# A gated-attention block with an MLP on one core: a fourth round of the second MLP product in three reduced passes, attention results parked in DRAM, and a new order of the work

## The chip, the cores and the metric

The kernel runs on one core of a Trainium2 chip. The metric is device time in microseconds (us) of one execution; lower is better. Kernels are compared by the median of several executions. The trace comes from one further, profiled execution.

## What is computed

The first half is a recurrent attention (four batches, eight heads, 768 time steps, 48 channels per head). Its output is laid out as 768 rows of 384 numbers per batch, and a normalized MLP with a residual follows, 384 to 1536 to 384.

```python
for t in range(S):
    kt, vt, rt, wt = (k[:, :, t], v[:, :, t], r[:, :, t], w[:, :, t])
    cur = np.einsum('bhd,bhe->bhde', u[None] * kt, vt)
    y[:, :, t] = np.einsum('bhd,bhde->bhe', rt, state + cur)
    state = wt[:, :, :, None] * state + np.einsum('bhd,bhe->bhde', kt, vt)
x = y.transpose(0, 2, 1, 3).reshape(B, S, H * D)
xn = (x - mu) / np.sqrt(var + 1e-06) * g_ln
out = x + np.maximum(xn @ w_ch1, 0.0) @ w_ch2
```

All inputs and outputs are 32-bit floats.

## The kernel before

The work is cut into eight rounds (four batches, two halves of 384 steps each). `front` (L1559) emits one round of attention: it loads w, k, r with `load` (L494, SyncE queue, three DMAs each), turns them with TensorE (`turn`), and then treats each chunk of 64 steps in six levels. At every level `quads` (L677) makes many small 48-row matmuls on quarters of the array, `grow` (L709) multiplies k and r by running products of w on VectorE, and `keep` copies the wanted squares out of PSUM on VectorE. `states` carries the state over the chunks, and `outputs` (L955) makes the attention result. Its last step on VectorE, `add` (L1006), writes the round's `x`, 128 x 3 x 384 numbers, 576 KB.

`back` (L1628) emits a round's MLP: `normalize` (L1030) on VectorE, `turn_x` (L1098) to transpose, and `mlp` (L1452). For rounds 1 to 7 the first product (`h_ps`, `hd_ps`) is made in three reduced-precision passes (type fp32r in the trace): the 32-bit numbers are split into a high and a low part and a correction, so that one 32-bit product is the sum of three passes. The third part of the weights, `d`, is streamed from DRAM for each of the twelve slices f of 128 hidden channels (`stream`, L1319). Round 0 uses plain 32-bit matmuls. The second product exists in two forms. Plain: for each third i of the round's rows, twelve 32-bit matmuls 128x128x384 into tile `o` (L1519 to L1555), one VectorE add (`x<-o,x`), and a store. In three passes: `thirds` (L1336), which splits h into `hH`, `hL`, `hD` (one ScalarE step, two VectorE steps per f), makes three fp32r matmuls per i and f against the split weights `w2h`, `w2l`, `w2d` that `halve2` (L1276) prepares once, and needs two VectorE steps per third at the end. `thirds` accumulates in six PSUM tiles, four of them in the two large "a" tiles that attention also uses, so it can only run when all attention is done: its first matmul waits for the `x` of the last round (L1414 to L1415). Before the change `LAST = NR - 3 = 5` (L427): rounds 5, 6 and 7 take three passes, rounds 0 to 4 are plain.

The order of the work is not the order of the text. Each step is added to a `Plan` (L67) with an engine, a cost, a due number (`pri`, smaller is more urgent), the tiles that it reads and writes, and how long after its end the result is usable (`lat`). `Plan.order` (L142) then simulates the engines and writes down one order per engine, which the chip follows strictly. `SHIFTS` (L90) moves the due numbers of single stages, and `PATIENCE`, `STAY`, `MARGIN`, `FETCH` and `WAIT` (L82 to L86) steer the choice: `STAY` is how many due numbers it is worth not to switch TensorE between the small 48-row matmuls and full-size ones. While TensorE has nothing to do in the first 90 us by the plan, `idle` matmuls are put in. Buffers are counted in `HOMES` (L330): three for `x`.

SyncE issues nearly all DMAs, in the plan's order; an entry that waits holds up all behind it.

Of the kernel before, what the change touches and what calls it, by code (L numbers as in the profile page):

```python
# [10 lines left out]
F32 = mybir.dt.float32  # L11
# [24 lines left out]
class InOrder:  # L36


    waits, last = [], None
# [27 lines left out]
class Plan:  # L67
# [11 lines left out]

    HOP, MARGIN, FILLED, PATIENCE, STAY = 0.1, 0.196918, 60.0, 4.33011, 6.79752  # L82
    BEFORE, PIECE, FETCH, CROWD = 66, 256, 3.98109, 300
    WAITS = 1.006
    DRAIN = {True: 0.1, False: 0.12}
    WAIT = {"PE": 0.0354766, "ACT": 0.217982, "DVE": 0.140393, "POOL": 0.485775, "SP": 0.0207245}  # L86

    SHIFTS = {  # L90
        -537: -0.5, -535: -6.5, -520: -4, -457: -8, -337: 9.5, -296: 10.5, -295: 5.5, -200: -2,
        -38: -71, -34: 42.5, -31: -47, -30: -6.5, -29: 16, -25: -3, -18: -10.5, -14: -56, 0:
        -25, 6: -19.5, 8: -4, 9: -2.5, 10: -43, 11: 16, 12: -24, 14: 3, 16: 18, 17: 31, 26: -27,
        46: 6.5, 50: -49, 52: 46.5, 61: -28.5, 64: 5.5, 66: 11, 68: -8, 86: 5.5, 91: -28, 96:
        -20.5, 98: -50, 102: 40.5, 110: 4.5, 121: -4, 122: 14, 125: -0.5, 127: -9, 131: -17.5,
        136: -30, 140: 24.5, 165: -9, 166: -6, 168: -11.5, 172: -40, 174: -34.5, 178: -1.5, 180:
        -14.5, 182: 25.5, 202: 4.5, 203: 37, 204: -10, 210: -66.5, 212: -41, 260: -1.5, 261:
        -16.5, 280: 30, 283: -13, 284: -4.5, 310: 5, 319: -7.5, 320: 9, 402: 6, 407: -20.5, 409:
        -6, 411: -30, 418: -9.5, 425: 2.5, 440: -68, 442: 5, 443: 5.5, 444: -9.5, 450: -20.5,
        453: 38, 459: -24, 463: 40.5, 480: 3.5, 481: 3, 483: 9.5, 486: -3.5, 490: 3.5, 495: 15,  # L100
        496: 18, 497: 17.5, 499: 64.5, 501: 5,
    }

    def __init__(self, homes, dynamic):
# [176 lines left out]
def kernel(  # L281
# [13 lines left out]
    PE, ACT, DVE, POOL, SP = (  # L295
        InOrder(tc, e) for e in (nc.tensor, nc.scalar, nc.vector, nc.gpsimd, nc.sync)
    )

    B, H, S, D = r.shape
    P = 128  # L300
# [5 lines left out]
    U = H // NH  # L306
    TT = 3
# [10 lines left out]
    NR = B * NHALF  # L318
    G = 3
    pairs, both_units = range(NP), range(U)  # L320
# [4 lines left out]
    scratch = ctx.enter_context(tc.tile_pool(name="scratch", bufs=1, space=DRAM))  # L325
# [3 lines left out]

    HOMES = {  # L330
        "nat": 5, "w": 1, "k": 2, "r": 2, "tot": 1, "decay": 3, "rk": 1, "own": 2, "own_row": 1,
        "v": 2, "vx": 2, "vo": 2, "s": 2, "last": 3, "rx": 2, "sx": 2, "x": 3, "xn": 3,
        "xf": 2, "stats": 2, "mv": 2, "rstd": 2, "raw": 4, "rest": 8, "h": 12, "w1": 4, "wl": 4,
        "w2": 12, "A": 2,
    }
# [3 lines left out]
    def tile_(tag, name, shape, dtype=F32):  # L339
        if name in tiles:  # L340
            return tiles[name]
        if tag == "a":
            tiles[name] = a_homes[plan.place[name]]
            return tiles[name]
        if tag == "nat" and name.startswith("nat_"):
            tiles[name] = nat_homes[plan.place[name]]
            return tiles[name]
        if tag == "b":
            t = banks.tile([P, 512], dtype, tag=f"b{plan.place[name]}", name=name)
            tiles[name] = t[:, 0 : shape[1]]  # L350
            return tiles[name]
        t = homes.tile(shape, dtype, tag=f"{tag}{plan.place[name]}", name=name)
        tiles[name] = t
        return t
# [25 lines left out]
    for i in range(2):  # L380
        plan.hold("A", f"A{i}")
        a_bufs.append(tile_("A", f"A{i}", [P, 2, U, NK, C]))
    own_d = [scratch.tile([RN, H], F32, name=f"own_d{i}") for i in range(ROWS)]
    w1_d = scratch.tile([FC, P, KC, P], F32, name="w1d")
    masks = [const.tile([P, C // 2], I8, name=f"mask{lev}") for lev in range(NLEV - 1)]
# [38 lines left out]

    BY = {"DVE": DVE, "POOL": POOL}
    EITHER = ("DVE", "POOL")
    THREE, LAST = 1, NR - 3  # L427

    def at(rnd, stage):
        return 40 * rnd + stage  # L430

    EVICT, CONVERT, FILL = -1000, 38, 200

# [8 lines left out]
    def urgent(part, stage):  # L444
        rnd, c0, nc = part
        return at(rnd - (nc == 1), stage)
# [47 lines left out]
    def load(nm, q):  # L494
        b, f, g = units[q]
        name = f"nat_{nm}{q}"

        def go():
            to = tile_("nat", name, None)
            if q // U < ROWS:  # L500
                SP.dma_start(
                    out=to[:, 0 : NH * ROW].rearrange("p (h x) -> p h x", h=NH),
                    in_=SRC[nm][b, ts(g, NH), ds(f * RN, RN)]
                    .rearrange("h (p c) d -> p h (c d)", p=P),
                )
                return
            for c in range(TT):
                SP.dma_start(
                    out=by_tile(to)[:, c, :, 0:D],
                    in_=SRC[nm][b, ts(g, NH), ds(f * RN + c * P, P)].rearrange("h p d -> p h d"),  # L510
                )

        cost_, size = (0.5, 1.05) if q // U < ROWS else (1.65, 1.6)
        plan.add(
            "SP", cost_, go, w=[name], new=[("nat", name)], pri=at(q // U, "wrk".index(nm)), lat=2.0,
            size=size,
        )

# [308 lines left out]
    def load_v(q, part):  # L827
        _, c0, nc = part
        b, f, g = units[q]
        name, swapped = f"v{q}", f"vx{q}"  # L830

        def go():
            t = tile_("v", name, [P, NH, TT, D])
            for c in range(c0, c0 + nc):
                SP.dma_start(
                    out=t[:, :, c],
                    in_=v[b, ts(g, NH), ds(f * RN + c * P, P)].rearrange("h p d -> p h d"),
                )

        def swap():  # L840
            t, src = tile_("vx", swapped, [P, NP, TT, D]), tiles[name]
            cols = slice(c0 * D, (c0 + nc) * D)
            for i in range(2):
                SP.dma_start(
                    out=t[ds(C * (1 - i), C)].rearrange("p r c d -> p r (c d)")[..., cols],
                    in_=src[ds(C * i, C)]
                    .rearrange("p (r j) c d -> p r j (c d)", j=2)[:, :, 1, cols],
                )

        share = nc / TT  # L850
        plan.add(
            "SP", 0.1 + 1.6 * share, go, w=[(name, c0)], new=[] if c0 else [("v", name)],
            pri=urgent(part, 16), lat=2.0, size=1.6 * share,
        )
        plan.add(
            "SP", 1.3, swap, r=[(name, c0)], w=[(swapped, c0)], new=[] if c0 else [("vx", swapped)],
            pri=urgent(part, 17), lat=2.2, size=0.2 + 0.5 * share,
        )
# [96 lines left out]
    def outputs(q, before, part):  # L955
        rnd, c0, nc = part
        uu = q % U
        b, f, g = units[q]
        y_, x_, sx, s_, rx = f"y{q}_{c0}", f"x{rnd}", f"sx{q}", f"s{q}", f"rx{q}"
        tiles_of = [(pr, c) for pr in pairs for c in range(c0, c0 + nc)]  # L960

        def go():
# [36 lines left out]
            + [(f"vx{q}", c0), (f"v{q}", c0), (s_, c0), (s_, 0)]  # L999
            + [(t, j, c0) for t in (rx, sx) for j in range(2)]  # L1000
            + keys_of("r", part, [uu]) + ([before] if before else []),
            w=[y_], new=[("a", y_)] + ([("x", x_)] if uu == c0 == 0 else []), pri=urgent(part, 24),
            lat=0.17, tiled=True, count=64 * nc - 16 * (before is None and c0 == 0),
        )
        for j in range(2):
            def add(j=j):  # L1006
                x = tile_("x", x_, [P, TT, H, D])
                y = tiles[y_][:, j, 0 : NK * D].rearrange("p (r c e) -> p r c e", r=NP, c=TT)
                cs = slice(c0, c0 + nc)
                DVE.tensor_tensor(  # L1010
                    out=x[:, cs, ts(g, NH)].rearrange("p c (r j) e -> p j r c e", j=2)[:, j],
                    in0=y[:, :, cs],
                    in1=tiles[f"vo{q}"].rearrange("p (r j) c e -> p j r c e", j=2)[:, j, :, cs],
                    op=ALU.add,
                )
            plan.add(
                "DVE", cost(part, 0.12, 0.41), add, r=[y_, (f"vo{q}", c0)], w=[(x_, uu, j, c0)],
                pri=urgent(part, 24),
            )

    def x_of(rnd, tile_no=None):

        return [
            (f"x{rnd}", uu, j, c0) for _, c0, nc in parts_of_round(rnd)
            if tile_no is None or c0 <= tile_no < c0 + nc for uu in both_units for j in range(2)
        ]
# [307 lines left out]
    def thirds(rnd, f):  # L1336
# [34 lines left out]
        for i in range(TT):  # L1371
# [40 lines left out]
            keys = [o + n if i == 2 else (o, n) for n in "PD"]  # L1412
            need = [H_, L_, D_, f"w2d{f}", (f"w2h{g}", c), (f"w2l{g}", c)]
            if first:  # L1414
                need += x_of(NR - 1)  # L1415
            plan.add(
                "PE", 0.525, both, count=6, r=need, w=keys,
                new=[("a" if i < 2 else "b", n) for n in names] if first else [],
# [140 lines left out]
    def front(part):  # L1559
# [59 lines left out]
        befores = [states(q, part) for q in qs]  # L1619
        for q, before in zip(qs, befores):  # L1620
            outputs(q, before, part)

    def norm(part):
        normalize(part)
        for kc in range(KC):
            turn_x(part, kc)

    def back(rnd):  # L1628
        norm((rnd, 0, TT))
        mlp(rnd)  # L1630

# [66 lines left out]
```

## Time and profile before

| | us |
|---|---|
| median of 3 runs | 527.17 |
| lowest, highest | 525.99, 527.70 |
| profiled execution | 526.92 |
| its span in the trace | 525.20 |
| TensorE busy | 515.8 |
| VectorE busy | 403.6 |
| ScalarE busy | 269.8 |
| GpSimd busy | 72.2 |

The profiled execution took 526.92 us, of which the trace spans 525.20; 1.72 us lie around the span. Busy time is the time in which at least one instruction of an engine runs. TensorE's instructions overlap in a pipeline, so a busy share near 100% does not say that every instruction went through as fast as it could; the distance from one start to the next tells that. Granted TensorE clock is 1.00 throughout.

### The profile page before, as it was taken

The numbers are of one execution on the slowest core, as the hardware profiler recorded it, in microseconds if no ns is written. First come the engines' busy times: TensorE is split into PE (matmuls) and PEld (weight loads), VectorE is DVE, ScalarE is ACT, GpSimd is POOL, SyncE is SP. The second block draws the span as 40 slices with busy tenths as digits, with TensorE's granted clock in tenths as the row PEclk, the third lists the DMA queues.
The fourth block names the chain that finished last, engine by engine and source line by source line (L and its number), as shares of the span: only waits on it lengthen the run. The fifth ranks groups of instructions, "written<-read, shape, count | busy, mean of one in ns | idle before, by whom it ended". The sixth has DMA issues, their size and how long they took to land.

```text
span 525.2 us, 20616 instructions
## 1 busy us (share of the span) xinstructions
PE 515.8 (98%) x8996; PEld 434.5 (83%) x8996; DVE 403.6 (77%) x845; ACT 269.8 (51%) x602; POOL 72.2 (14%) x106
## 2 busy tenths in 40 slices
PE   9999999999999999999999999999999999999996
PEld 6788788677998668989777898669967999999996
DVE  5899988998899998999893886736664855855645
ACT  3788978973584244385451395246731524332221
POOL 7311311100420012223120010001500000000000
PEclk9999999999999999999999999999999999999999
DMA  9958595087545724655712311404101322322201
GB/s 215 273 158 205 119 232 163 18 208 209 143 83 102 187 50 93 145 121 102 174 39 67 78 38 25 133 22 120 47 16 61 107 61 65 101 60 85 83 0 46
DMA packets 122362, 55.84 MB, mean 106 GB/s; under 512 B 93984, under 2 KB 119200, under 8 KB 122272
## 3 DMA queue, kind: packets, MB, share of 16 engines
q1 hardware_dynamic: 119152, 53.54, 40.3%
q10 hardware_dynamic: 3120, 0.98, 1.0%
q8 instruction: 71, 1.16, 0.9%
q14 instruction: 19, 0.16, 0.1%
HBM read 45.05 MB, written 7.10 MB: 99 GB/s over the span
## 4 chain that ended last, share of the span: by engine, by line
PE 88%; DMA 4%; DVE 3%; POOL 2%; ACT 1%; issue 0%; SPq 0%; POOLq 0%; DVEq 0%
PE a L50 24%; PE o L50 23%; PE h_ps L50 21%; PE hd_ps L50 9%; PE o_2P L50 2%; PE w_ps L50 2%; PE r_ps L50 2%; DMA nat<-in_w_dram 2%; PE kn_ps L50 2%; PE k_ps L50 2%; PE xT_ps L50 1%; PE o_2D L50 1%; DVE x L50 1%; DMA own<-own_d 1%; DVE w L50 1%; POOL wide L50 1%
## 5 line engine op out<-in xcount | busy, mean ns | idle before, releaser
L50 PE MATMUL o<-ffn,h 128*128 128x384 f32 x360 | 124.4, 490 | 0.0
L50 PEld LDWEIGHTS o<-ffn,h 128*128 128x128 f32 x360 | 65.7, 190 | 37.5
L50 ACT COPY h<-hd_ps 128x384 f32<-128x384 f32 x84 | 40.3, 479 | 80.0 <-PE hd_ps L50 77.4
L50 DVE SCALAR_TENSOR_TENSOR h<-h_ps,h 128x384 f32<-128x384 f32 x84 | 46.5, 555 | 42.1 <-PE h_ps L50 38.1
L50 PEld LDWEIGHTS a<-r,k 48*60 48x60 f32 (+5 forms) x4608 | 63.3, 126 | 15.4 <-issue 7.4
L50 PE MATMUL a<-r,k 48*60 48x32 f32 (+5 forms) x4608 | 69.6, 212 | 0.9 <-issue 0.6
L50 PE MATMUL h_ps<-xhl,wl 128*128 128x384 f32 x252 | 61.1, 350 | 0.0
L50 PE MATMUL h_ps<-xhl,wh 128*128 128x384 f32 x252 | 57.6, 337 | 0.0
L50 PE MATMUL hd_ps<-xd,d 128*128 128x384 f32 x252 | 57.2, 348 | 0.0
L50 DVE TENSOR_TENSOR k<-k,tot 112x768 f32<-112x768 f32 (+1 forms) x50 | 41.7, 833 | 16.7 <-PE a L50 13.9
L50 PEld LDWEIGHTS hd_ps<-xd,d 128*128 128x128 f32 x252 | 44.2, 188 | 1.6 <-ACT w L50 0.2
L50 PEld LDWEIGHTS h_ps<-xhl,wl 128*128 128x128 f32 x252 | 43.8, 188 | 1.8 <-DVE h L50 0.2
L50 PEld LDWEIGHTS h_ps<-xhl,wh 128*128 128x128 f32 x252 | 45.2, 188 | 0.0
L50 ACT ACTIVATE h<-h 128x384 f32<-128x384 f32 x48 | 25.1, 525 | 33.3 <-DVE h L50 32.7
L50 DVE TENSOR_TENSOR r<-r,tot 112x768 f32<-112x768 f32 (+1 forms) x50 | 40.3, 807 | 0.0
L50 DVE COPY_PREDICATED A<-mask,a 128x768 f32<-128x768 int8 (+2 forms) x36 | 39.3, 1091 | 0.5 <-PE a L50 0.3
L50 ACT ACTIVATE hH<-h 128x384 fp32r<-128x384 f32 x36 | 18.4, 524 | 30.2 <-DVE h L50 25.8
L50 ACT COPY A<-a 32x384 f32<-32x384 f32 (+2 forms) x36 | 15.5, 432 | 26.9 <-PE a L50 25.7
L50 DVE SCALAR_TENSOR_TENSOR hL<-h,hH 128x384 fp32r<-128x384 f32 x36 | 19.9, 553 | 9.8 <-ACT hH L50 9.7
L50 PE MATMUL h_ps<-xf,w 128*128 128x128 f32 (+1 forms) x144 | 26.2, 331 | 0.0
L50 PE MATMUL a<-w2d,hD 128*128 128x384 f32 x72 | 24.6, 342 | 0.7 <-DVE hD L50 0.7
L50 PEld LDWEIGHTS a<-v,A 64*64 64x64 f32 x384 | 20.5, 133 | 5.4 <-issue 2.0
(121 smaller groups left out, 1000.8 us busy)
## 6 DMA issues: line engine op xcount, KB each, us to landing
d<-w1d SPq DMA_DIRECT2D x84, 192.0 KB, 2.9
raw<-in_moe_w_ch_dram SPq DMA_DIRECT2D x24, 384.0 KB, 4.7
v<-in_v_dram SPq DMA_DIRECT2D x48, 96.0 KB, 2.8
out_dram<-x SPq DMA_DIRECT2D x24, 192.0 KB, 1.9
nat<-in_w_dram SPq DMA_DIRECT2D x36, 96.0 KB, 3.5
nat<-in_k_dram SPq DMA_DIRECT2D x36, 96.0 KB, 3.6
nat<-in_r_dram SPq DMA_DIRECT2D x36, 96.0 KB, 3.1
w1d<-w1diff SPq DMA_DIRECT2D x12, 192.0 KB, 2.7
```

Source lines behind the costliest of these rows:

```text
L50: ins = self.tc.keep_in_program_order(f(*args, **kw))
```

## The change

- `LAST` becomes `NR - 4 = 4`: rounds 4 to 7 make the second product in three passes.
- New constant `APART = 3`. For rounds 3 to 7, attention writes its result into a tile `early` (one buffer, tag "y"), and a new step `aside` on the SyncE queue stores it to DRAM (`x_d`, 576 KB a round). Before such a round is normalized, a new step `again` loads it into an `x` tile. `HOMES` has two buffers for `x` instead of three, and one for `y`.
- The first three-pass matmul waits for the landing of the last round's `aside` store.
- The plan counts the loads of w, k, r of rounds from 2 on with 1.95 us of queue time instead of 1.65 and 2.5 us to landing instead of 2.0, and the loads of v with 2.5 us instead of 2.0. These numbers steer the order only.
- `FILL`, the due number of MLP filling work, goes from 200 to 240.
- The steering constants and the table of shifts are new.

```diff
-    HOP, MARGIN, FILLED, PATIENCE, STAY = 0.1, 0.196918, 60.0, 4.33011, 6.79752
-    BEFORE, PIECE, FETCH, CROWD = 66, 256, 3.98109, 300
+    HOP, MARGIN, FILLED, PATIENCE, STAY = 0.1, 0.05, 60.0, 12.9046, 22.5969
+    BEFORE, PIECE, FETCH, CROWD = 66, 256, 3.89769, 300
...
-    WAIT = {"PE": 0.0354766, "ACT": 0.217982, "DVE": 0.140393, "POOL": 0.485775, "SP": 0.0207245}
+    WAIT = {"PE": 0.0114264, "ACT": 0.145789, "DVE": 0.235109, "POOL": 0.433917, "SP": 0.0810123}
...
     SHIFTS = {
-        -537: -0.5, -535: -6.5, -520: -4, -457: -8, -337: 9.5, -296: 10.5, -295: 5.5, -200: -2,
...
+        -472: -7.5, -375: -15, -38: -7, -32: -4.5, -29: -18.5, -26: -23, -24: 16.5, -20: -2, 1:
...
-        "v": 2, "vx": 2, "vo": 2, "s": 2, "last": 3, "rx": 2, "sx": 2, "x": 3, "xn": 3,
+        "v": 2, "vx": 2, "vo": 2, "s": 2, "last": 3, "rx": 2, "sx": 2, "x": 2, "y": 1, "xn": 3,
...
+    x_d = scratch.tile([NR, P, TT * H * D], F32, name="x_d")
...
-    THREE, LAST = 1, NR - 3
+
+    APART = 3
+    THREE, LAST = 1, NR - 4
...
-    EVICT, CONVERT, FILL = -1000, 38, 200
+    EVICT, CONVERT, FILL = -1000, 38, 240
...
-        cost_, size = (0.5, 1.05) if q // U < ROWS else (1.65, 1.6)
+        cost_, size = (0.5, 1.05) if q // U < ROWS else (1.95, 1.6)
...
-            pri=urgent(part, 16), lat=2.0, size=1.6 * share,
+            pri=urgent(part, 16), lat=2.5, size=1.6 * share,
...
+        x_ = f"x{rnd}" if rnd < APART else f"early{rnd}"
...
+    def aside(rnd):
+        x_ = f"early{rnd}"
+
+        def go():
+            SP.dma_start(out=x_d[rnd], in_=tiles[x_].rearrange("p c h d -> p (c h d)"))
+
+        plan.add(
+            "SP", 0.4, go, r=[(x_, uu, j, 0) for uu in both_units for j in range(2)],
+            w=[("x_d", rnd)], pri=at(rnd, 25), lat=2.8, size=1.9,
+        )
+
+    def again(rnd):
+        x_ = f"x{rnd}"
+
+        def go():
+            t = tile_("x", x_, [P, TT, H, D])
+            SP.dma_start(out=t.rearrange("p c h d -> p (c h d)"), in_=x_d[rnd])
+
+        plan.add(
+            "SP", 0.4, go, r=[("x_d", rnd)], w=x_of(rnd), new=[("x", x_)], pri=at(rnd, 25), lat=2.0,
+            size=1.7,
+        )
...
             if first:
-                need += x_of(NR - 1)
+                need += [("x_d", NR - 1)]
...
+        if rnd >= APART:
+            aside(rnd)
...
     def back(rnd):
+        if rnd >= APART:
+            again(rnd)
         norm((rnd, 0, TT))
         mlp(rnd)
```

## The prediction

> **What bounds the kernel now.** I read the page first, for the share of each engine over time.
>
> ```profile
> PE 515.8 (98%) x8996; PEld 434.5 (83%) x8996; DVE 403.6 (77%) x845; ACT 269.8 (51%) x602; POOL 72.2 (14%) x106
> ...
> PE   9999999999999999999999999999999999999996
> ...
> DVE  5899988998899998999893886736664855855645
> ```
>
> TensorE is busy in every slice but the last; VectorE is close to full only up to about slice 22 (290 us). A busy TensorE may still be held up between matmuls, so I looked at what it waited for, and at the chain that ended last.
>
> ```profile
> PE idle L50 <- DVE eps L50: 1.0, 1, 1.0
> PE r_ps L50 <- DMA nat<-in_r_dram: 0.7, 1, 0.7
> PE w_ps L50 <- ACT held L50: 0.7, 1, 0.7
> PE a L50 <- DVE hD L50: 0.7, 1, 0.7
> ```
>
> These are the longest waits of TensorE: about 5 us in all. The chain in order of time gives prices that count start to start:
>
> ```profile
> 189.16 2.13 PE o L50 x6
> ...
> 194.11 1.95 PE o L50 x6
> ...
> 383.40 17.42 PE o L50 x54
> ...
> 440.04 2.09 PE h_ps L50 x12
> ...
> 515.25 1.06 PE a L50 x6
> ```
>
> "o" is the plain second product; each 32-bit matmul leaves two records, so 54 records are 27 matmuls: 17.42 / 27 = 0.645 us each. "h_ps" and the late "a" are reduced passes, one record each: 0.175 us. The row of 2.13 follows attention's small matmuls, that of 1.95 doesn't: a switch back costs 0.18 to 0.19 us.
>
> Adding up, over all records of TensorE, by how much a start-to-start distance exceeds the middle one of its kind (where by over 0.15 us), I get 10.2 us of hold-ups: 7.0 before 75 us, 1.4 just after 400 us (0.8 of it ahead of the first three-pass matmul), 1.8 between. About 5 us at the end are VectorE and the last store. So the time is TensorE's work plus some 15 us; a change pays by what it takes from that work, if it adds no wait.
>
> Is VectorE near to being a second bound? By windows of the attention part (busy us of PE, PEld, DVE, ACT, POOL) and of the MLP tail:
>
> ```profile
> 100.00:150.00 50.00, 50.00 (x958) 39.75 (x958) 45.26 (x89) 31.05 (x71) 8.58 (x9) 1.00 0.65 162
> 150.00:200.00 50.00, 50.00 (x1153) 37.78 (x1153) 47.22 (x105) 21.00 (x47) 6.20 (x8) 1.00 0.46 104
> 200.00:250.00 50.00, 50.00 (x1425) 44.83 (x1424) 46.07 (x96) 29.78 (x68) 9.84 (x12) 1.00 0.57 117
> ...
> 407.00:525.20 118.20, 112.87 (x674) 111.77 (x664) 74.94 (x149) 39.07 (x82) 1.02 (x1) 1.00 0.22 68
> ```
>
> VectorE held 91 to 94% for 150 us and TensorE never ran dry; in the tail VectorE is at 63%.
>
> **What the Trainium skill says.** "FP8 and Floating Point Precision", TensorE Precision Notes: a true 32-bit product is four passes. The trace agrees roughly: 0.645 / 0.175 = 3.7. "TensorEngine Tiling (Array Packing)", Key Properties: a change of the tiling mode drains the engine; the trace shows about 0.19 us on the way back to full size. "DMA: Bandwidth & Descriptors", Anatomy of one DMA: about 2.0 us plus bytes over 436 GB/s, fitted for the GpSimd path; for 576 KB (589,824 bytes) that is an estimate of 3.4 us. The trace has only neighbours on this queue: 192 KB stores of x at 1.9 us, 384 KB weight loads at 4.7 us.
>
> **The change, part by part.**
>
> *Round 4's second product.* Out: 36 plain matmuls, 36 x 0.645 = 23.2 us. In: 108 passes, 108 x 0.175 = 18.9 us. TensorE: -4.3 us, all of it on the path.
>
> *Its VectorE steps.* 12 hL at 553 ns and 12 hD at 556 ns are new: 13.3 us; three adds `x<-o,x` (554) become six: +1.7 us. ScalarE swaps one relu (525 ns) for one hH (524). These 15 us run in the tail, 118 us long before and some 165 us long after. By the changed order VectorE has about 108 us of rows behind attention's last add: 66%, near the 63% of now. On the path: nothing. If the cover is gone, a 0.56 us step that is late costs that much.
>
> *The tail needs attention to end earlier.* Behind the last attention matmul the changed order has four rounds of first product (36 x 3 x 0.175 x 2 = 37.8 us for first plus second product, 151 us together), six leftover plain "o" (3.9) and 27 transposes (about 3): 158 us, where before it had 112. So attention must be over at about 358 us instead of 407, with less MLP work to lie beside it. I gave each row of the changed order the mean busy time of its kind in this trace and added up by engine: up to the last attention step VectorE has 310 us, TensorE 344. From the end of round 2 to the end of round 7 it is 164.2 against 187.7, so VectorE needs 87.5%; the same sums for the order before are 186.5 against 212.5, 87.8%. In the densest part (round 2 to round 5) it is 101 against 111, 91%, what the windows above show it can hold. I take nothing for it; the other end is rival B.
>
> *Fewer switches.* By the orders, attention's small matmuls and full-size ones alternate 77 times instead of 82: 5 x 0.19 = -1.0 us (the way into the small ones would add to that; not counted).
>
> *Idle fillers.* 19 instead of 18 rows of idle matmuls; at the means of their kinds 12.1 against 11.1 us: +1.0 us at most, nothing if they stand in waits that would be there anyway. I take +1.0.
>
> *x through DRAM.* Five stores and five loads of 576 KB, 5.9 MB on 55.8 moved (+11%); the DMA engines are 22% busy in the tail, 42 to 65% in attention. Ten more issues on SyncE's queue at 0.34 us (the row of the x stores). No TensorE or VectorE work. Landing: 1.9 us (the 192 KB store) to 7 us (the 384 KB load's 4.7 times 1.5); I take 3.5. Waits: (a) The first three-pass matmul waits for the landing of round 7's store. In the order 12.0 us of other matmuls stand between the last attention matmul and it (3.2 before); the chain is four x adds (1.8), issue (0.34), landing (3.5): 5.6, so hidden, and the 0.8 us hold-up of before should go or stay small. (b) A reload waits for the stores of the x two rounds earlier, then normalization follows. Chain for round 6: two VectorE steps (1.1), issue and store (0.34 + 1.9), issue and load (0.34 + 3.5), statistics, root and apply (1.5 + 0.3 + 0.4 + 0.2 + 1.3 = 3.7): 10.9 us; in the order 17.7 us of TensorE work lie between the last product of round 4 and round 6's transposes, 17.2 for round 5, 19.8 for round 7. Covered by 6 to 9 us; at a landing of 7 us and 4.2 for the store (its maximum in the trace), by 0.5 to 3. Behind an unlanded load stand VectorE's split steps (statistics come first in its order) and on SyncE the `d` slices, which eight buffers (about 25 us of tail work) keep ahead. Cost 0; other end 1 to 1.5 us for each of three reloads. (c) One `early` buffer: rounds lie some 40 us apart, so it is free.
>
> *Loads planned longer, FILL, shifts.* They move loads earlier in SyncE's order, past stores and slices; no instruction is added. What can be gained is the 0.7 us wait of "r_ps" and part of the 7.0 us before 75 us, what can be lost is a like amount. I take 0.
>
> Sum: -4.3 - 1.0 + 1.0 = -4.3 us. The profiled execution of 526.92 (span 525.20 and 1.72 around it) becomes 522.6; it lies 0.25 below the median of 527.17, which gives 522.9. I put 522.8. As a check from the whole: rows by means give TensorE 509.5 before and 505.4 after, -4.1.
>
> **The rivals.** A is the forecast: 521 to 525.6.
>
> B, slower: VectorE cannot hold 87.5% under the shorter attention part, since its steps and TensorE's wait for each other level by level, and with fewer plain products to lie between, TensorE runs dry. For it: over 156 to 344 us the trace has VectorE at 156.91 of 188 us, 83.5%. At that share the 164.2 us take 196.6, 8.9 more than TensorE's 187.7: 526.9 - 4.3 + 8.9 = 531.5. It decides from a share below 164.2 / (187.7 + 4.3) = 85.5%. Against it: the same ratio (87.8%) stood in the order before without a dry spell, and in that window TensorE, not VectorE, was full.
>
> C, the gain is spent on new waits: reloads that come 1 to 1.5 us late three times, or early-phase hold-ups that grow by 3 to 4 us: 526 to 527. For it: in-order queues. Against it: the cushions above.
>
> D, more than the forecast: the new order also takes away half of the 7.0 us before 75 us: 519. For it: those are waits for loads and VectorE, which an order can change; against it: the first rows of the order hardly differ.
>
> That three passes are not made in round 4 is excluded: the order has 144 plain "o" matmuls instead of 180, and 432 passes instead of 324.
>
> **How the numbers follow.** A 0.53, D 0.15, C 0.17 (most of it within 0.3%, some below), B 0.15. A measurement of this kernel can tell about 0.3%, 1.6 us: faster is below 525.6, slower above 528.8. Faster: A, D and a little of C, 0.73; same 0.14; slower 0.13, for B has cases below 528.8. Range 518.5 to 528.5, which leaves out most of B and a sliver of D.
>
> **What would show it.** Right: "o" falls to 288 records at 0.32 us start to start, late "a" and "o_2" passes rise to 432; TensorE's waits stay near 5 us; the last attention add lies near 358 us (409.8 now); VectorE is at about 87% before and 66% after it; no wait of "xT_ps" or of statistics for `x_d`. Wrong: "a" matmuls waiting for VectorE's k or A between 150 and 350 us (B), waits for the reload around 370, 415 and 450 us or a longer first 75 us (C).

## The result and the profile after

| | before | after |
|---|---|---|
| median (20 runs each), us | 527.14 | 524.53 |
| lowest, highest, us | 525.81, 530.20 | 522.47, 528.43 |
| ratio of the two, 95% interval | | 0.9944 [0.9929, 0.9960] |
| a second comparison, on another chip (13 and 6 runs), us | 527.27 | 522.92 |
| its ratio, 95% interval | | 0.9917 [0.9896, 0.9938] |
| profiled execution, us | 526.92 | 524.47 |
| its span, us | 525.20 | 522.70 |

The changed kernel is faster: by 2.6 us in the first comparison and by 4.4 in the second. The forecast was 522.8, 4.3 less than the kernel before. In some experiments below, single executions took over 1.5% longer than the fastest of the same kernel; the ratios leave these out, the medians do not.

The page of the changed kernel: the busy times, the rows of TensorE and VectorE over the span in 40 slices, the granted clock, and the group of plain second products.

```profile
PE 511.3 (98%) x9034; PEld 439.8 (84%) x9034; DVE 417.1 (80%) x875; ACT 268.1 (51%) x602; POOL 68.3 (13%) x103
...
PE   9999899999999999999999999999999999999996
...
DVE  5888989999989997898996889757775688776555
...
PEclk9999999999999999999999999999999999999999
...
L50 PE MATMUL o<-ffn,h 128*128 128x384 f32 x288 | 101.1, 492 | 0.0
```

TensorE's busy time fell by 4.5 us (515.8 before), VectorE's rose by 13.5 (403.6), and TensorE is as full as it was. The plain product has 288 records, so one round's 36 matmuls are gone. One slice of TensorE now shows an 8, the fifth (52 to 65 us).

Its waits (us in all, times, longest):

```profile
PE a L50 <- issue: 2.1, 3, 1.4
PE idle L50 <- DVE eps L50: 1.0, 1, 1.0
PE k_ps L50 <- ACT w L50: 1.0, 1, 1.0
PE a L50 <- DVE hD L50: 0.9, 1, 0.9
PE r_ps L50 <- DMA nat<-in_r_dram: 0.8, 1, 0.8
PE a L50 <- DVE A L50: 0.4, 1, 0.4
```

They add up to 6.2 us, 1.6 more than the eight waits of before (4.6). The first row has grown: it was 0.6 us in two waits of at most 0.3, and is now 1.4 us at once. "issue" means that nothing the profile knows of held the matmul up. The wait for `hD` near the start of the three-pass products was to go or stay small; it has gone from 0.7 to 0.9 us.

The transfers through DRAM (issue duration min/median/max, first and last start; who waited; time to landing):

```profile
L50 SPq DMA_DIRECT2D x_d<-early x5: 347/448/508, 196.9 to 361.6; - x5
L50 SPq DMA_DIRECT2D x<-x_d x5: 319/320/327, 221.4 to 448.6; - x5
...
who waited for it (us, times):
  POOL rk L50: 1.4, 1
  DVE stats L50: 0.6, 1
...
DMA to landing us min/median/max: 3.5/3.9/5.0
```

No matmul waits for them. They land after 3.9 us in the middle, where 3.5 was taken. VectorE's last step of attention, an add into `early`, starts at 358.7 us (358 forecast); its store is issued at 361.6, behind five loads of `d` on SyncE's queue.

The stretches (busy us of PE, PEld, DVE, ACT, POOL; granted clock; DMA share; GB/s):

```profile
75.00:150.00 75.00, 74.95 (x1688) 59.20 (x1688) 68.73 (x128) 46.77 (x107) 10.52 (x11) 1.00 0.59 150
150.00:200.00 50.00, 49.86 (x1334) 39.98 (x1321) 45.23 (x105) 28.08 (x65) 14.41 (x17) 1.00 0.57 125
200.00:250.00 50.00, 49.43 (x1316) 42.23 (x1315) 44.28 (x84) 24.66 (x56) 7.51 (x8) 1.00 0.64 143
250.00:300.00 50.00, 49.92 (x1210) 37.05 (x1209) 41.42 (x72) 19.77 (x44) 2.83 (x3) 1.00 0.32 84
300.00:362.00 62.00, 62.00 (x1252) 49.45 (x1251) 47.87 (x116) 37.37 (x84) 7.97 (x10) 1.00 0.27 74
362.00:522.70 160.70, 154.86 (x891) 153.60 (x889) 109.23 (x220) 54.80 (x116) 0.00 (x0) 1.00 0.27 84
```

VectorE holds 92, 90, 89, 83 and 77% while TensorE stays full; in the tail it is at 68% (66 forecast).

**Where the time went.** I gave every TensorE record, except the idle fillers, the middle start-to-start distance of its kind in the trace before (for the small matmuls, the mean of the distances below 250 ns), and call the sum useful work and the rest of the span lost.

| us | before | after | difference |
|---|---|---|---|
| useful work | 485.8 | 481.5 | -4.3 |
| lost | 39.4 | 41.2 | +1.8 |
| span | 525.2 | 522.7 | -2.5 |
| lost up to 75 us | 23.6 | 24.0 | +0.4 |
| lost up to 350 us | 32.5 | 35.1 | +2.6 |
| lost up to 380 us | 33.3 | 36.4 | +3.1 |
| lost up to 420 us | 34.4 | 36.4 | +2.0 |

The work fell by the forecast's 4.3 us. This only counts records at the prices of before; that the prices hold in the changed kernel, and that the product is the gain, is shown further down. What falls short is in the loss. By kinds: switches back to full size 20.1 to 19.15 us (77 instead of 82, -0.95; forecast -1.0); idle fillers, start to start, 13.6 to 15.85 (+2.3; forecast +1.0 at most); hold-ups by the prediction's own count 10.2 to 11.0 (+0.8); small overruns within the blocks of small matmuls 4.7 to 5.6 (+0.9). These kinds overlap (a filler that is held up counts twice), so they do not add up to 1.8.

### The profile page after: what moved, and what is told of

It is laid out like the page before. It is cut to its first block, busy times and chain, and to the rows that moved or that the text cites. A ratio compares the mean times of both kernels' runs of the same rounds, so it can differ in the third digit from the quotient of the medians.

```text
span 522.7 us, 20737 instructions
## 1 busy us (share of the span) xinstructions
PE 511.3 (98%) x9034; PEld 439.8 (84%) x9034; DVE 417.1 (80%) x875; ACT 268.1 (51%) x602; POOL 68.3 (13%) x103
## 3 DMA queue, kind: packets, MB, share of 16 engines
q8 instruction: 71, 1.16, 1.0%
## 4 chain that ended last, share of the span: by engine, by line
PE 90%; DMA 3%; DVE 3%; ACT 2%; issue 1%; SPq 1%; POOL 0%; DVEq 0%
PE a L50 27%; PE h_ps L50 22%; PE o L50 17%; PE hd_ps L50 9%; PE o_2P L50 3%; PE r_ps L50 2%; PE k_ps L50 2%; DMA nat<-in_r_dram 2%; PE kn_ps L50 2%; PE w_ps L50 2%; PE xT_ps L50 2%; PE o_2D L50 1%; DMA nat<-in_w_dram 1%; PE idle L50 1%; ACT w L50 1%
## 5 line engine op out<-in xcount | busy, mean ns | idle before, releaser
L50 PE MATMUL o<-ffn,h 128*128 128x384 f32 x288 | 101.1, 492 | 0.0
L50 ACT COPY h<-hd_ps 128x384 f32<-128x384 f32 x84 | 40.3, 480 | 88.4 <-PE hd_ps L50 85.5
L50 PEld LDWEIGHTS a<-r,k 48*63 48x63 f32 (+5 forms) x4608 | 63.2, 126 | 16.3 <-issue 7.2
L50 PEld LDWEIGHTS o<-ffn,h 128*128 128x128 f32 x288 | 51.8, 190 | 28.2
L50 DVE SCALAR_TENSOR_TENSOR h<-h_ps,h 128x384 f32<-128x384 f32 x84 | 46.4, 555 | 29.6 <-PE h_ps L50 27.1
L50 PE MATMUL a<-r,k 48*63 48x32 f32 (+5 forms) x4608 | 69.1, 212 | 0.7 <-issue 0.7
L50 PE MATMUL h_ps<-xhl,wl 128*128 128x384 f32 x252 | 59.4, 344 | 0.0
L50 PE MATMUL h_ps<-xhl,wh 128*128 128x384 f32 x252 | 57.7, 337 | 0.0
L50 PE MATMUL hd_ps<-xd,d 128*128 128x384 f32 x252 | 57.0, 347 | 0.0
L50 DVE TENSOR_TENSOR k<-k,tot 112x768 f32<-112x768 f32 (+1 forms) x50 | 41.0, 820 | 10.1 <-PE a L50 9.0
L50 PEld LDWEIGHTS hd_ps<-xd,d 128*128 128x128 f32 x252 | 44.3, 188 | 1.7 <-ACT w L50 0.2
L50 PEld LDWEIGHTS h_ps<-xhl,wh 128*128 128x128 f32 x252 | 45.2, 188 | 0.0
L50 PEld LDWEIGHTS h_ps<-xhl,wl 128*128 128x128 f32 x252 | 44.2, 188 | 0.9 <-DVE h L50 0.3
L50 ACT ACTIVATE hH<-h 128x384 fp32r<-128x384 f32 x48 | 24.7, 524 | 35.3 <-DVE h L50 26.5
L50 DVE COPY_PREDICATED A<-mask,a 128x768 f32<-128x768 int8 (+2 forms) x36 | 39.3, 1094 | 1.7 <-PE a L50 1.4
L50 DVE TENSOR_TENSOR r<-r,tot 112x768 f32<-112x768 f32 (+1 forms) x50 | 39.7, 794 | 0.0
L50 DVE SCALAR_TENSOR_TENSOR hL<-h,hH 128x384 fp32r<-128x384 f32 x48 | 26.7, 555 | 15.0 <-ACT hH L50 14.6
L50 PE MATMUL a<-w2d,hD 128*128 128x384 f32 x96 | 32.9, 343 | 0.9 <-DVE hD L50 0.9
L50 PE MATMUL a<-w2l,hL 128*128 128x384 f32 x96 | 32.3, 337 | 0.0
L50 PE MATMUL a<-w2h,hH 128*128 128x384 f32 x96 | 32.2, 336 | 0.0
L50 ACT ACTIVATE h<-h 128x384 f32<-128x384 f32 x36 | 18.7, 526 | 23.7 <-DVE h L50 23.5
L50 DVE SCALAR_TENSOR_TENSOR hD<-hH,hL 128x384 fp32r<-128x384 f32 x48 | 26.7, 555 | 1.2
```

Source lines behind the costliest of these rows:

```text
L50: ins = self.tc.keep_in_program_order(f(*args, **kw))
```

## The experiments

Theory 1 is the forecast's: the time is TensorE's work, the second product of round 4 carries the gain, the rest is hidden. Theory 2, its rivals: VectorE is nearly a second bound (B), or the transfers and the new order take back part of the gain (C). Ratios are to the kernel before, measured on the same chip at the same time. Where nothing else is said, the order of the instructions is that of the changed kernel.

### The plain product back in round 4

```diff
+                if rnd == LAST:
+                    PE.matmul(
+                        out_tiles(i)[0], tiles[D_][:, ts(i, P)].bitcast(F32),
+                        tiles[f"w2d{f}"].bitcast(F32), start=first, stop=last,
+                    )
+                    return
...
-                    out=x, in0=out_tiles(i)[1].rearrange("p (h d) -> p h d", d=D), in1=x, op=ALU.add
+                    out=x, in0=out_tiles(i)[rnd > LAST].rearrange("p (h d) -> p h d", d=D), in1=x, op=ALU.add
```

> The changed kernel's order, kept as it is, with one thing undone: in round 4 each three reduced passes of the second product (3 x 0.175 us) are replaced by one 32-bit matmul (0.645 us) of the correction parts hD and w2d. Left out of the computation: the main parts of round 4's second product. Theory 1 (TensorE's work sets the time, and the product is what gained): 36 x 0.12 = 4.3 us slower than the changed kernel, about 528.8 us, a little above the kernel before. Rival (the gain came from the new order, and round 4's passes stand beside other waits): within 1.5 us of the changed kernel's 524.5.

526.94 us, ratio 1.0004 [0.9983, 1.0025]: no faster than the kernel before. Against the changed kernel it is 1.0004 / 0.9944 = 1.006 or 1.0004 / 0.9917 = 1.009, 3.2 to 4.6 us slower. On its page:

```profile
PE 514.7 (98%) x8998; PEld 434.5 (83%) x8998; DVE 415.9 (79%) x875; ACT 268.3 (51%) x602; POOL 69.1 (13%) x103
...
L50 PE MATMUL a<-w2d,hD 128*128 128x384 f32 x120 | 43.4, 405 | 0.5 <-DVE hD L50 0.5
```

TensorE's busy time is 3.4 us up with 36 records fewer, and the group now mixes 72 passes of the other three rounds with 48 records of 32-bit matmuls. DRAM detour, splits and order are those of the changed kernel, and with them alone nothing is won: to within about 1 us the product is the whole gain.

### Stores and loads of x doubled

```diff
+            SP.dma_start(out=x_e[rnd], in_=tiles[x_].rearrange("p c h d -> p (c h d)"))
...
+            SP.dma_start(out=x_f[rnd], in_=x_d[rnd])
```

The first stands in `aside`, the second, a copy within DRAM, in `again` ahead of the load.

> The changed kernel's order with the traffic of x through DRAM doubled: each of the five stores is issued twice (the second to another DRAM buffer), and each of the five loads is preceded by a DRAM-to-DRAM copy of the same 576 KB. Theory 1 (the detour is covered by other work): within 1.5 us of 524.5. Rival (the detour's queue time, landings and contention have eaten part of the gain): 1.5 to 4 us slower than the changed kernel, 526 to 528.5.

529.95 us, ratio 1.0054 [1.0028, 1.0081], which fits neither theory. And it isn't clean: 2.4 us more than in the changed kernel were lost before 75 us, ahead of the first doubled store at about 197 us, where a load of `r` came late ("PE r_ps L50 <- DMA nat<-in_r_dram: 3.1, 3, 2.8" among its waits). It was repeated below on another base.

### No idle fillers

```diff
-        while n:
+        while n and False:
```

> The changed kernel's order without the idle matmuls that the plan puts into TensorE's free time in the first 90 us (15.8 us of start-to-start time in the trace of the changed kernel, 13.6 in that before). Theory 1 (they stand in waits that are there anyway): within 1.5 us of 524.5. Rival 1 (they delay real work; the 2.3 us more of them is where the missing gain went): 2 us or more faster, 522 or less. Rival 2 (they keep TensorE's clock up): slower by some us, and a lower granted clock in the first slices.

531.04 us, ratio 1.0069 [1.0035, 1.0102], so some 6.6 us slower than with them. The page:

```profile
PE   6789799999999999999999999999999999999996
...
PEclk9759799999999999999999999999999999999999
```

Without fillers TensorE's clock is granted at 0.7, 0.5 and 0.7 in slices 2, 3 and 5 (13 to 40 and 53 to 66 us), 0.976 over the run. So the 2.3 us more that fillers take in the changed kernel are no price that could simply be saved. How much of the 6.6 us is the clock isn't separated, though. The edit also takes 78 records from TensorE, and their count matters by itself, as the last experiment shows: waits for "issue" add up to 6.6 us in this trace, against 2.1 in that of the changed kernel, and the second drop of the clock begins at 58.1 us, within such a wait of 1.5 us.

### VectorE's own-term sums made twice, in both kernels

14 reductions of 0.74 us in rounds 1 to 7, 10.4 us more of VectorE's work; the same edit in the changed kernel and in the one before.

```diff
-            DVE.tensor_reduce(out=t[:, :, ds(h0, heads)], in_=parts()[2], axis=AX.X, op=ALU.add)
+            for _ in range(2 if rnd else 1):
+                DVE.tensor_reduce(out=t[:, :, ds(h0, heads)], in_=parts()[2], axis=AX.X, op=ALU.add)
```

> The changed kernel's order with 10.4 us more of VectorE in the attention part: in rounds 1 to 7 the sum of the own term (0.74 us each, 14 of them) is made twice with the same result. Theory 1 (TensorE sets the time and VectorE has room): under 2 us slower than 524.5. Rival B (VectorE has become a second bound of the shortened attention part): 5 to 10 us slower, 529.5 to 535. To be set beside the same edit of the kernel before.

> The kernel before, with the same 10.4 us more of VectorE in attention (14 sums of 0.74 us made twice, same result, same order). Theory 1: under 2 us slower than the 527.1 of the kernel before, and about as much slower as the changed kernel gets from it. Rival B (the change has used up VectorE's room): clearly less slower here than in the changed kernel, by 3 us or more.

In the changed kernel 523.46 us, ratio 0.9926 [0.9896, 0.9955]: not slower than without the edit (0.9944 and 0.9917). In the kernel before 529.33, ratio 1.0051 [1.0031, 1.0072], 2.3 us slower. The stretch of 75 to 300 us of the changed kernel with the edit:

```profile
75.00:300.00 225.00, 223.58 (x5507) 178.25 (x5500) 206.97 (x399) 119.17 (x269) 36.74 (x40) 1.00 0.52 127
```

VectorE is at 206.97 / 225 = 92% for 225 us (199.66 without the edit, 89%) and the time stands still. Over the run its busy time rose by 8.2 us, to 425.3. Rival B is out: there was room for these 14 steps in the part where it was thought to bind. That the kernel before did pay 2.3 us is the reverse of what B has to expect; its trace does not name one place for it, but 1.3 us of it stand in longer waits for "issue" (1.9 against 0.6), the subject of the last experiment.

### Other orders: five rounds plain, and the two plans exchanged

Three kernels whose order the planner makes anew. The changed kernel with three-pass products in three rounds only:

```diff
-    THREE, LAST = 1, NR - 4
+    THREE, LAST = 1, NR - 3
```

The changed kernel with the steering numbers, shifts, `FILL` and load times of before, and the kernel before with those of the changed one (the diff is of the first; the second is its mirror image):

```diff
-    HOP, MARGIN, FILLED, PATIENCE, STAY = 0.1, 0.05, 60.0, 12.9046, 22.5969
+    HOP, MARGIN, FILLED, PATIENCE, STAY = 0.1, 0.196918, 60.0, 4.33011, 6.79752
...
-    EVICT, CONVERT, FILL = -1000, 38, 240
+    EVICT, CONVERT, FILL = -1000, 38, 200
```

> The changed kernel with three rounds in three passes again (5 to 7), all else as changed: x through DRAM, load times, shifts. The plan makes another order from it. Theory 1 (the fourth round gains 4.3 us, the rest is about neutral or slightly bad): 527.5 to 531. Rival (the new shifts and load times made the gain): 524 to 526.

> The changed kernel with the plan's numbers of before (steering constants, shifts, FILL, load times); four rounds in three passes and x through DRAM stay. The plan makes another order. Theory 1 (work gives -4.3 us, but only an order fitted to the new structure keeps waits off TensorE): slower than 524.5, since the old shifts were found for other due numbers: 526 to 540. Rival (the product alone carries the gain, the order matters little): 523 to 525.5.

> The kernel before with the plan's numbers of after (constants, shifts, FILL, load times), three rounds in three passes, x kept in SBUF. Theory 1: as slow as or slower than 527.1, since the shifts were found for another structure: 527 to 540. Rival (the new numbers are better in themselves): 524 to 526.

| | us | ratio |
|---|---|---|
| changed structure, three rounds in three passes | 536.17 | 1.0176 [1.0146, 1.0205] |
| changed structure, plan of before | 540.47 | 1.0226 [1.0191, 1.0262] |
| structure of before, plan of after | 534.11 | 1.0139 [1.0105, 1.0174] |

All are slower than both kernels, the first by more than either theory allowed. In its waits one row is new in size, and it lies in the tail, in three waits between 416 and 468 us:

```profile
PE a L50 <- DVE hD L50: 4.1, 3, 1.9
```

A set of shifts fits one structure; on another it costs 7 to 16 us, more than the change brings. So these three cannot tell what the plan alone is worth: half the change with the other half's plan is not half the change. They do show that the structure alone, with the old plan, loses.

### The changed kernel again, and u's load moved behind k's

In the changed kernel the second early load of `r`, on ScalarE's queue, is issued at 6.7 us and lands at 14.4; in the kernel before at 4.3 and 10.6. In SyncE's order `u`'s load (192 KB) stands ahead of the second part of k's load in the changed kernel, and behind it before. The edit puts it behind; all else keeps its order.

```diff
-    for fn in plan.order(busy, ("b", 0.24, idle), 90.0):
+    fns = plan.order(busy, ("b", 0.24, idle), 90.0)
+    u_load = firsts["u"].out
+    fns.remove(u_load)
+    fns.insert(fns.index(firsts["k", 1].out) + 1, u_load)
+    for fn in fns:
```

> The changed kernel itself again, as the control for the runs beside it: 0.994 of the kernel before, about 524.

> The changed kernel with one DMA moved: the load of u (192 KB, spread to all partitions) is issued behind the load of k for the second part of round 0, as in the kernel before, and not ahead of it; every engine's order is otherwise the same. Theory L (part of the gain is lost because round 0's last load of r, issued at 4.3 us and landed at 10.6 us before, is now issued at 6.4 to 6.7 us and lands at 12.4 to 14.9 us, so that TensorE runs dry near 14 us and its clock may drop): r lands near 11 to 12 us in every profile and the time falls by 1 to 2.5 us below the control. Rival (the early loads don't matter, the shortfall is spread over attention): within 0.8 us of the control.

Changed kernel 522.92, ratio 0.9917 [0.9896, 0.9938]; with the moved load 522.37, ratio 0.9917 [0.9897, 0.9936]. `r` then lands at 11.0 us and the hold-up of about 0.9 us at 13.4 us is gone from the trace, yet no difference can be measured. The lowest median of all kernels here, and no better than the changed kernel by any interval.

### The detour doubled on this base

The edit of the second experiment, on top of the moved load.

> The kernel with the load of u moved, and the traffic of x through DRAM doubled (each store twice, each load preceded by a DRAM-to-DRAM copy of its 576 KB). Theory (the doubling itself costs little; the 5.8 us that it seemed to cost came partly from the early loads, ahead of the first doubled store): under 3 us slower than the kernel with u moved alone, with the loss only behind 190 us in the trace. Rival (the detour costs about 5 us per doubling): 4.5 us or more slower.

530.68 us, ratio 1.0069 [1.0044, 1.0094], 8 us more than its base. The answer for `x_d`, and VectorE's timeline around 380 us (start, duration, then in brackets the idle time ahead and what ended it):

```profile
  DVE stats L50: 4.5, 4
...
DMA to landing us min/median/max: 4.4/5.6/6.1
```

```profile
377.60 0.56 DVE L50 SCALAR_TENSOR_TENSOR hD<-hH,hL 128x384 fp32r<-128x384 f32 x1
380.07 1.02 DVE L50 BATCH_NORM_STATS2 stats<-x 128x6 f32<-128x384 f32 x2 [1.92 <-DMA x<-x_d]
...
382.15 0.55 DVE L50 SCALAR_TENSOR_TENSOR hL<-h,hH 128x384 fp32r<-128x384 f32 x1
382.73 0.56 DVE L50 SCALAR_TENSOR_TENSOR hD<-hH,hL 128x384 fp32r<-128x384 f32 x1
```

Here is rival C's chain: the statistics wait for the reload, the splits `hL` and `hD` stand behind them in VectorE's order, and TensorE waits 2.9 us for `hD`, 2.0 more than in the base. That is a quarter of the 8 us. Set against the same records in the trace of its base, this one falls behind in two other places: by about 4 us between 245 and 262 us of the base, and by 1.7 between 300 and 320. Both are "issue" hold-ups, treated next: 1.8 us of idle time up to 248.5 us (0.5 in the base), with the clock granted at 0.5 for 6.8 us from there, and 1.2 us up to 311.6 (none in the base). So the 8 us have the size that the rival named, but three quarters of them are not the detour's chain. Whether the doubled traffic makes those holds longer isn't shown: with the same traffic the second experiment's trace has 0.2 and 0.5 us at these two places. With a single detour the statistics waited for 0 to 0.6 us in the seven traces of this order. So one detour just fits and two do not; the cost of two says nothing about that of one. No run takes the detour away in this order, so what a single one costs isn't measured.

### The "issue" hold: 48 more records of TensorE

Numbering all of TensorE's records in order (matmuls, weight loads and its 139 semaphore and drain instructions), the holds that the profile ascribes to "issue" in the changed kernel stand where the number is 192 more than a multiple of 256. The timeline of the changed kernel around 55 us:

```profile
54.76 0.22 PE L50 MATMUL a<-sx,rx 48*64 48x48 f32 x1
54.77 0.28 PE L50 MATMUL a<-s,r 48*64 48x48 f32 x3
56.49 0.31 PE L50 MATMUL a<-sx,rx 48*64 48x48 f32 x3 [1.45 <-issue]
```

The hold lies in the middle of a run of equal small matmuls, at record 2240, and records 1984 to 2240 were issued in 1.89 us. The edit makes the first filler 18 matmuls of 128 columns instead of 6 of 384, so that all later records count 48 higher. (It is on top of the moved load.)

```diff
+    waits, last, started = [], None, False
...
+        fine = not InOrder.started
+        InOrder.started = True
...
-            now = min(n, TT)
+            now = 1 if fine else min(n, TT)
```

> The kernel with the load of u moved, and TensorE's first idle filler written as 18 matmuls of 128 columns in place of 6 of 384: the same columns, 48 more instruction records ahead of all else. Theory F (holds at every 256th instruction of TensorE are refills of its instruction stream; the one at 54.8 us, after 256 instructions in 1.9 us, comes from where the boundary falls): the hold at the record number 2240 is gone or moves by 48 records to 2240 again in the count, that is to an earlier matmul, and becomes shorter, 0.5 to 1.5 us faster than with u moved alone. Rival (the hold belongs to that matmul, not to a record count): it stays at the same matmul, same time.

536.67 us, ratio 1.0179 [1.0151, 1.0206]: 14 us slower than its base, where the theory had a gain. The timeline and the clock row:

```profile
123.83 2.83 PE L50 MATMUL a<-r,k 48*63 48x32 f32 x184
128.91 0.43 PE L50 MATMUL a<-r,k 48*62 48x32 f32 x8 [2.25 <-issue]
129.27 0.89 PE L50 MATMUL w_ps<-ident,nat 128*112 128x128 f32 x3
129.95 4.05 PE L50 MATMUL o<-ffn,h 128*128 128x384 f32 x6
```

```profile
PEclk9999999997999999899899999999999999999999
```

The mechanism held, its sign did not. At record 2240, now an earlier matmul, 0.7 us of hold remain; but boundaries moved into other dense runs: at 109, 126, 172, 220 and 258 us, 256 records were issued in 1.6 to 2.3 us, and holds of 1.35 to 2.45 us follow. After the one at 126 us six plain records take 4.05 us instead of 1.94, since the clock is granted at half. Added up over all boundaries the holds are 10.6 us against 3.3 in its base, and the rest goes with a lower clock (0.986 over the span). So where these boundaries fall is a property of an order that no due number shows, and the changed kernel's order, with one hold of over 1 us, is a good one.

## Why the prediction was right

*Round 4's product, -4.3.* Right: useful work fell by 4.3, and with the plain product put back the gain is gone. The prices hold in the changed kernel's chain in order of time (start, duration, records):

```profile
99.08 1.95 PE o L50 x6
102.30 2.13 PE o L50 x6
...
513.58 2.10 PE a L50 x12
```

Six plain records take 1.95 us, 0.325 each (2.13 behind small matmuls, a switch of 0.18), and twelve passes 2.10, 0.175 each.

*Switches, -1.0.* Right: 77, and -0.95.

*VectorE's 15 us, nothing.* Right: busy time rose by 13.5, the tail stands at 68%, and the doubled sums in the attention part cost nothing measurable. Up to 362 us VectorE held 85% (87 forecast). Rival B let the share that VectorE reached in one stretch (83.5%) stand for the most that it can reach. From the end of round 2 to that of round 7 (168.0 to 359.2 us) the changed kernel has VectorE at 161.14 of 191.20 us, 84%, below B's point of decision, with TensorE at 190.55: VectorE was lower because less was asked of it.

One reason against B was wrong, however. The prediction gave the order before the same share, 186.5 against 212.5 us, 87.8%. In the trace before, that stretch runs from 166.2 to 410.2 us, with VectorE at 185.41 of 244.00 us, 76%: the first of the two sums fits, the second doesn't. So the change did ask for a larger share of VectorE there than before. What carried the forecast were the windows at 91 to 94%; this comparison was no support, and that it did no harm is luck.

*x through DRAM, nothing.* Right as far as it can be seen: no wait of TensorE names it, and it lands as estimated. But the cushions of 6 to 9 us were too generous in one point. I counted them up to the transposes of the reload's own round; the next `hL` and `hD` of VectorE, which I named as standing behind it, are only a few us away. VectorE's timeline of the changed kernel, and the matmul that waits for its last row, before and after:

```profile
372.60 1.02 DVE L50 BATCH_NORM_STATS2 stats<-x 128x6 f32<-128x384 f32 x2
...
374.68 0.55 DVE L50 SCALAR_TENSOR_TENSOR hL<-h,hH 128x384 fp32r<-128x384 f32 x1
375.26 0.56 DVE L50 SCALAR_TENSOR_TENSOR hD<-hH,hL 128x384 fp32r<-128x384 f32 x1
```

```profile
418.08 0.45 PE L50 MATMUL a<-w2d,hD 128*128 128x384 f32 x1 [0.65 <-DVE hD L50]
```

```profile
375.88 0.45 PE L50 MATMUL a<-w2d,hD 128*128 128x384 f32 x1 [0.93 <-DVE hD L50]
```

The statistics have their `x` in time, yet the splits behind them are late for TensorE. I had put the 0.8 us of before ahead of the first three-pass matmul and counted the chain through the last store, which did have room. That was a misreading: the first three-pass matmul starts at 410.6 us before and at 370.1 after, and waits for nothing in either. The hold stands ahead of the third slice's, and what it waits for is VectorE's order. From the start of the matmul ahead of it to its own pass 0.99 us before and 1.26 after, so the hold neither went nor stayed: it grew by 0.3.

*Fillers, +1.0 at most.* Missized: +2.3. I took means over rows, which already fell short of the trace before (11.1 against 13.6 us start to start); the changed order's have more of the long ones (28 records of 384 columns instead of 24), and the last comes at 52 us instead of 33. But it is not 1.3 us more on the path, for the loss up to 75 us grew by 0.4 only: where fillers grew, other waits went. That was rival D's idea, and all it gave was to pay for the fillers.

*Loads and shifts, nothing.* Missized by little: the hold-ups grew by 0.8, a 1.66 us hold at an instruction boundary (TensorE's longest) against waits that went.

Of the 1.8 us more that were lost, not all belongs to the change. The order up to 358 us is the same in the kernel with the plain product put back, yet up to 350 us that one lost 32.5 us, as much as the kernel before, the changed kernel 35.1, its repetition 35.5 and the one with doubled sums 33.1. Traces of one order differ by 3 us there, and the two comparisons (-2.6 and -4.4) differ as much. Which of the early holds makes it long or short in an execution stays open: moving the late load of `r` settled one of them and changed no median.

## What to carry to other kernels

Where one engine is full, count its work start to start and price a change by what it takes from that: here this gave -4.3 us, where -2.6 and -4.4 were measured, while another engine at 92% cost nothing. When you ask what waits for a new transfer, follow the waiting engine's own queue to the next step, whoever's it is, before you follow the data. An order found by search fits one program down to the count of its instructions; judge a change of structure only with an order of its own, and change one thing in a fixed order to find out what it is worth.

## What the runs showed of the hardware

TensorE stops at boundaries of 256 records (semaphore instructions counted in) when the records before were issued fast. The Trainium skill, "Runtime: NRT & Kernel Launch", section "Instruction fetch mechanics", says that instructions are fetched in blocks of 16 KiB, 256 of them, and that crossing into the next is mostly hidden. The block size fits: the profile's page counts 71 packets and 1.16 MB on the instruction queue, and TensorE's 18,207 records are 71.1 blocks. Hidden it is not always. In the traces of this study every block but one that was issued in less than 2.4 us was followed by a hold, of 0.7 to 2.45 us. Of the blocks that took 3 to 5 us most had none, some up to 1.1 us, and three 1.35, 1.7 and 1.97 us. The length is not fixed by the block: after the same records 1984 to 2240, issued in 1.9 us, nine traces have 1.2 to 1.8 us. That it is the fetch is inferred from the count and the queue; that the place goes by the count of records was shown by moving it.

The granted clock can fall after such a hold, as it does without fillers: 0.5 in the 5 us after the hold at 126 us of the kernel with 48 more records, where six records of the plain product took 4.05 us instead of 1.94. After the 1.66 us hold of the changed kernel it stayed at 1.00. In all traces of this study the drops to 0.5, but for those at a program's end, begin during an idle time of TensorE of 1.2 to 2.8 us or within 2 us after it, and last 3.4 or 6.8 us, one 17.1. Idle times of 1.2 to 2.9 us without a drop stand beside them, so their length alone does not decide; what does stays open.
